# S4 convolution and attention: SP's transfers in the program's order, and other tiles over the bytes that transfers still read

## The chip, the cores and the metric

The kernel runs on one NeuronCore of a Trainium2 chip. The metric is the device time of one execution in microseconds (us); for a kernel that is run several times, the median. The core has these engines: TensorE (PE) multiplies matrices into PSUM, VectorE (DVE) and ScalarE (ACT) work on SBUF and PSUM, GpSimd (POOL) fills constants and issues some transfers, SyncE (SP) issues most of the DMA transfers. Each engine works through its own list of instructions in order and waits on semaphores.

## The reference, cut to what matters

Four layers, each added to its input: an S4 convolution (A), an attention with 32 query heads on one key and value head (B), and both again with the same parameters.

```python
def A(u, A_re, A_im, B_re, B_im, C_re, C_im, log_dt, Dskip):     # u: [1, 2048, 640]
    dt = exp(log_dt)[:, None]                                     # 640 channels, 128 states
    P = exp((dt * (A_re + 1j*A_im))[:, :, None] * arange(2048))
    K = einsum("dn,dnl,dn->dl", C_re + 1j*C_im, P, dt * (B_re + 1j*B_im)).real
    y = irfft(rfft(pad(u.T)) * rfft(pad(K)))[:, :2048].T          # causal convolution
    return y + u * Dskip
x = x + A(layernorm(x), ...)
x = x + B(layernorm(x), ...)      # softmax attention, 2048 x 2048, 32 heads of 20
x = x + A(layernorm(x), ...)
x = x + B(layernorm(x), ...)
```

## The kernel before, in words

The program has these stages in order: the generation of the convolution's kernels `K` (`_kgen`), the first convolution (names with `a`), attention (`b`), the second convolution (`c`), attention (`d`). The change touches the generation, and how the convolutions name their memory and load their weights.

**Tables** (`kg_tables`, L161 to L260). From the parameters, which are loaded as [128, 5, 128] tiles, DVE and ACT compute for every channel and state an angle `th`, its fraction `thr`, 32 times that (`th1`), a decay `are`, a phase `ph` and a logarithm of a size `lw`. Each of `th1`, `thr`, `are`, `ph`, `lw` is split into three bf16 parts, in a tile `h...` of [128, 3, 5, 128]: `cast` makes a part, `rest` subtracts it. PE needs them with 16 channels per group as rows, stacked: `tb` has the three parts of `th1` in 48 rows, `ta` has `thr` in rows 0 to 47 and `ph` in rows 48 to 95, `tm` has `are` and `lw` in the same way. Two ways of transfer bring them there:

- `send` (L183): one store of the tile to DRAM (`hd...`, L185) and, when that has landed, three loads of 16 rows each (L187). So go `th1` to `tb`, `thr` to `ta`, `are` to `tm`.
- the late ones (L292 to L297): for each of the 8 groups of 16 partitions of `hph` and of `hlw`, three transfers of 20 KB, straight into rows 48 to 95 of group `q` in `ta` and `tm`. These are 48 transfers, in the profile `ta<-hph` and `tm<-hlw`.

**Units** (L302 on). 20 units of work each take 32 channels: unit `u` reads group `u % 8` of the tables (`grp`). For a unit PE makes two phases (L324: the first from `tb`, the second from `ta`), DVE takes their fraction (`r` L149, `f` L329), ACT makes sines and cosines (`trig`, L342 to L344). PE makes three sizes (`sizes` L352: two from rows 0 to 47 of `tm`, the third from all 96), ACT takes their exponential into `m1` and `m2` (`exps`, L360 and L362). DVE multiplies (`products`, L370 to L379), PE sums over the states (`sums`, L388), ACT collects the sums in `kst` (`store`, L396). When `kst` is full, four transfers bring it to DRAM in `kd` (L404, L408).

**What sets the order.** The instructions of DVE, ACT and PE in this stage stand in the order in which the program writes them (`manual_schedule`). SP's are not among them: a planner at build time puts them in an order by its own estimate of when each is ready, and it also pulls later transfers forward, such as the loads of x (`load_x`, L531, written at unit 0). Each DMA of SP takes the next of eight semaphores and waits until the transfer that used it before has landed. The order in the loop for unit 0 on PE is: both phases of unit 0, two sizes of unit 0, the first phase of unit 1, the second phase of unit 1, the third size of unit 0. The PSUM buffer of the phases is single, that of the sizes double.

**Memory.** The tables' tiles lie in a pool `kgq`; when it closes, the pool `kgb` of the units takes the same bytes, and after that the convolution's pool `cvp`. Tiles get their bytes in the order in which the program names them (one set of buffers per tag). The first instruction that writes a tile waits until all that used its bytes before are done, transfers that read them included. In `kgq` the `h` tiles come late: each is named in `kg_tables`, after 25 other tiles. In `kgb` the order is `r` (2 buffers), `f` (4), `c1`, `s1` (2 each), `fa`, `c2`, `s2` (3 each), `m1` (3), `m2`, `e1r` (2 each), `kst`. In `cvp` it is `xn` (3 buffers; the kernel `kt` is one of them), `dsk`, `A` (3), `zs`, the scratch `B` and `R`, the inverse weights `wi`.

**Convolution** (`conv_layer`, L596). Per chunk of 128 channels: the kernel is loaded from `kd` (L588; in the second layer its spectrum `kh`, L585), the input is normalized on ACT (`xn`, L605), `fwd` multiplies with the weights `wf` on PE (L512: step `t` reads the parts `t + 4` and `t`) and does the rest of the transform on DVE with the scratch `B`, `R` (`fft8`). The weights are loaded in eight parts of 512 KB (L493).

Of the kernel before, what the change touches and what calls it, by code (L numbers as in the profile page):

```python
# [11 lines left out]
F32 = mybir.dt.float32  # L12
F32R = mybir.dt.float32r
BF16 = mybir.dt.bfloat16
# [7 lines left out]
P = 128  # L22
L = 2048
D = 640
NST = 128
# [92 lines left out]
class Net:  # L118
# [39 lines left out]
        with ExitStack() as ctx:  # L158
            self._kgen(ctx)

    def kg_tables(self, pp, t3, SH, ldt, aim, are_raw, bre, bim, cre, cim, ta, tb, tm):  # L161

        nc = self.nc
        V, S, T, A = (nc.vector.tensor_tensor, nc.vector.scalar_tensor_tensor, nc.vector.tensor_scalar,
                      nc.scalar.activation)
        dt, th, are, thr, th1, ph = pp.tile([P, 5], F32, name="dt"), *(
            t3(n) for n in ("th", "are", "thr", "th1", "ph"))
        wr, wi, u0, u1, u2, u3, lw = (t3(n) for n in ("wr", "wi", "u0", "u1", "u2", "u3", "lw"))  # L170
        ar, ai, mx, mn, gt = (t3(n) for n in ("ar", "ai", "mx", "mn", "gt"))
        hs, res = {}, {}
        for n in ("th1", "thr", "are", "ph", "lw"):
            hs[n] = pp.tile([P, 3, 5, NST], BF16, name="h" + n)
            res[n] = t3("res" + n)

        def cast(n, src, k):
            A(hs[n][:, k], src if k == 0 else res[n], AF.Copy)

        def rest(n, src, k):  # L180
            V(res[n], src if k == 0 else res[n], hs[n][:, k], ALU.subtract)

        def send(n, dst):  # L183
            hd = self.dr.tile([P, 3, 5 * NST], BF16, name="hd" + n)
            nc.sync.dma_start(hd, hs[n].rearrange("p k t s -> p k (t s)"))  # L185
            for k in range(3):
                nc.sync.dma_start(dst[16 * k : 16 * k + 16].rearrange("d q t s -> d q (t s)"),  # L187
                                  hd[:, k].rearrange("(q d) x -> d q x", d=16))

        A(dt, ldt, AF.Exp)  # L190
        for t in range(5):
            T(th[:, t], aim[:, t], dt[:, t : t + 1], 1.0 / TWO_PI, ALU.mult, ALU.mult)
        V(wr, cre, bre, ALU.mult)
        self.frac(pp, thr, th, SH)
        T(th1, thr, 32.0, None, ALU.mult)
        self.frac(pp, th1, th1, SH)
        cast("th1", th1, 0)
        V(u0, cim, bim, ALU.mult)
        V(wr, wr, u0, ALU.subtract)
        A(ar, wr, AF.Abs)  # L200
        V(wi, cre, bim, ALU.mult)
        V(u0, cim, bre, ALU.mult)
        V(wi, wi, u0, ALU.add)
        A(ai, wi, AF.Abs)
        rest("th1", th1, 0)
        cast("th1", th1, 1)
        V(mx, ar, ai, ALU.max)
        V(mn, ar, ai, ALU.min)
        T(mx, mx, 1e-37, None, ALU.max)
        rest("th1", th1, 1)  # L210
        cast("th1", th1, 2)
        send("th1", tb)
        cast("thr", thr, 0)
        nc.vector.reciprocal(u0, mx)
        V(u0, mn, u0, ALU.mult)
        for t in range(5):
            A(are[:, t], are_raw[:, t], AF.Copy, scale=dt[:, t : t + 1])
        cast("are", are, 0)

        A(u1, u0, AF.Arctan)  # L220
        V(gt, ai, ar, ALU.is_gt)
        rest("thr", thr, 0)
        cast("thr", thr, 1)
        T(wr, wr, 0.0, 0.5, ALU.is_lt, ALU.mult)
        S(u1, gt, 0.5 * math.pi, u1, op0=ALU.mult, op1=ALU.subtract)
        A(u1, u1, AF.Abs, scale=1.0 / TWO_PI)
        T(wi, wi, 0.0, -2.0, ALU.is_lt, ALU.mult)
        rest("thr", thr, 1)
        V(u1, wr, u1, ALU.subtract)
        A(u1, u1, AF.Abs)  # L230
        cast("thr", thr, 2)
        send("thr", ta)
        T(ph, th1, 32.0, None, ALU.mult)
        self.frac(pp, ph, ph, SH)
        S(u1, wi, 1.0, u1, op0=ALU.add, op1=ALU.mult)
        V(ph, ph, u1, ALU.add)
        self.frac(pp, ph, ph, SH)

        A(u2, u0, AF.Square)
        A(lw, mx, AF.Ln)  # L240
        A(u3, u2, AF.Ln, bias=1.0)
        nc.vector.tensor_copy(hs["ph"][:, 0], ph)
        rest("ph", ph, 0)
        nc.vector.tensor_copy(hs["ph"][:, 1], res["ph"])
        rest("ph", ph, 1)
        nc.vector.tensor_copy(hs["ph"][:, 2], res["ph"])
        rest("are", are, 0)
        cast("are", are, 1)
        S(lw, u3, 0.5, lw, op0=ALU.mult, op1=ALU.add)
        for t in range(5):  # L250
            T(lw[:, t], lw[:, t], ldt[:, t : t + 1], None, ALU.add)
        rest("are", are, 1)
        cast("are", are, 2)
        send("are", tm)
        nc.vector.tensor_copy(hs["lw"][:, 0], lw)
        rest("lw", lw, 0)
        nc.vector.tensor_copy(hs["lw"][:, 1], res["lw"])
        rest("lw", lw, 1)
        nc.vector.tensor_copy(hs["lw"][:, 2], res["lw"])
        return (ta, hs["ph"]), (tm, hs["lw"])  # L260

    def _kgen(self, ctx):
        tc, nc, ins = self.tc, self.nc, self.ins
# [10 lines left out]
        with tc.tile_pool(name="kgq", bufs=1) as pp:  # L274
            SH = [P, 5, NST]

            def t3(name):
                return pp.tile(SH, F32, name=name)

            ldt = pp.tile([P, 5], F32, name="ldt")  # L280
            nc.sync.dma_start(ldt, ins["A_log_dt"])
            raw = {}
            for n, eng in (("A_A_im", nc.sync), ("A_C_re", nc.scalar), ("A_B_re", nc.sync),
                           ("A_C_im", nc.scalar), ("A_B_im", nc.sync), ("A_A_re", nc.scalar)):
                raw[n] = t3("r" + n)
                eng.dma_start(raw[n], ins[n].rearrange("(t p) n -> p t n", p=P))
            nc.sync.dma_start(kg, ins["c_kg"])
            bre, bim, cre, cim = (raw["A_" + n] for n in ("B_re", "B_im", "C_re", "C_im"))
            with tc.manual_schedule(engines={mybir.EngineType.Activation, mybir.EngineType.DVE}):
                late = self.kg_tables(pp, t3, SH, ldt, raw["A_A_im"], raw["A_A_re"], bre, bim, cre, cim,  # L290
                                      ta, tb, tm)
            for q in range(8):  # L292
                for dst, h in late:
                    for k in range(3):
                        nc.sync.dma_start(
                            dst[48 + 16 * k : 64 + 16 * k, q].rearrange("d t s -> d (t s)"),
                            h[16 * q : 16 * q + 16, k].rearrange("d t s -> d (t s)"))  # L297

        bp = ctx.enter_context(tc.tile_pool(name="kgb", bufs=2, reuse_waits="tile"))

# [1 line left out]
        units = [(q, r, q * 256 + 16 * r, 128, 128) for q in range(2) for r in range(8)]  # L302
        units += [(2, r, 512 + 16 * r, 64, 64) for r in range(4)]
        C1, S1, C2, S2, M1, M2, E1R, F, PE_, PK, KST = ({} for _ in range(11))

        def big(tag, u, x, bufs=2):
            return bp.tile([P, 16, 2, x], F32, tag=tag, bufs=bufs, name=f"{tag}_{u}")
# [82 lines left out]

        def store(u):
            q, r, _, _, run = units[u]
            if r == 0:
                KST[q] = bp.tile([P, 32, run], F32, tag="kst", bufs=1, name=f"kst{q}")
            kst = KST[q]
            nc.scalar.activation(kst[:, :, 16 * r : 16 * r + 16],  # L396
                                 PK[u].rearrange("p (d j) -> p j d", d=16), AF.Copy)
            if 16 * (r + 1) == run:
                for par in range(2):
                    for jh in range(2):  # L400
                        src = kst[64 * par : 64 * par + 64, 16 * jh : 16 * jh + 16, :]
                        if run == 128:
                            dst = self.kd[2 * q + par, 64 * jh : 64 * jh + 64]
                            nc.sync.dma_start(dst, src.rearrange("p t d -> p (t d)"))  # L404
                        else:
                            dst = self.kd[4, 64 * jh : 64 * jh + 64].rearrange(
                                "p (t d) -> p t d", d=DC)[:, :, 64 * par : 64 * par + 64]
                            nc.sync.dma_start(dst, src)  # L408
# [68 lines left out]
    def conv_setup(self, ctx):  # L477
# [2 lines left out]
            self.conv_weights(self.nc.sync)  # L480
        self.cvp = ctx.enter_context(tc.tile_pool(name="cvp", bufs=1, reuse_waits="tile"))

    def conv_weights(self, eng):

        stack = ExitStack()
# [3 lines left out]
        self.wfs.append(stack)  # L489

    def load_weights(self, w, name, eng):
        for t in range(8):
            eng.dma_start(w[:, t].rearrange("p a b c k -> p (a b c k)"),  # L493
                          self.ins[name][:, t * 1024 : (t + 1) * 1024])

    def scratch(self, nm):
        cv = self.cvp
        return (cv.tile([P, 16, 256], F32, tag="B", bufs=1, name=f"B{nm}"),
                cv.tile([P, 8, 256], F32, tag="R", bufs=1, name=f"R{nm}"))
# [560 lines left out]
```

## Time and profile before

| | us |
|---|---|
| Median of 3 runs (3184.24 to 3188.92) | 3187.74 |
| The profiled execution's own time | 3188.56 |
| Its span, first to last instruction | 3186.5 |
| First matmul of the generation (L324) | starts at 31.89 |
| First sum collected (L396) | starts at 101.60 |
| First matmul of the first convolution (L512) | starts at 367.13 |

The times in the trace count from the first instruction. The difference between the profiled execution's time and its span lies outside the instructions. In a row of the timeline, the brackets behind an instruction hold how long its engine stood idle before it and what ended that; `<-` in a tile's place separates what is written from what is read. `x3` counts instructions that the view has merged. `SPq` is SP's list of DMA issues: the duration there is that of the issue, not of the transfer.

### The profile page before, as it was taken

How to read it: one execution, taken by the hardware profiler on the slowest of the kernel's cores; microseconds unless marked ns; L12 is line 12 of the kernel's file. 1: busy time of each engine (PE TensorE's matmuls, PEld its weight loads, DVE VectorE, ACT ScalarE, POOL GpSimd, SP SyncE). 2: the span in 40 equal slices, each digit the busy share in tenths (PEclk: the TensorE clock that was granted, in tenths of full speed). 3: DMA queues.
4: the chain of work that ended last, by engine and by line, in shares of the span. 5: the costliest groups of instructions: out<-in, count | busy, mean ns of one | idle time of the engine just before them, and what ended most of it. 6: DMA issues, size and time to landing. Idle time of an engine off the chain costs nothing. (4 is left out here: it accounts for less than half of the span.)

```text
span 3186.5 us, 51392 instructions
## 1 busy us (share of the span) xinstructions
PE 2790.6 (88%) x21374; PEld 1315.3 (41%) x21374; DVE 1375.5 (43%) x1699; ACT 2335.3 (73%) x2703; POOL 13.1 (0%) x60
## 2 busy tenths in 40 slices
PE   1888776649899999999999867388999999999999
PEld 0555676647522233333333467365222333333334
DVE  6888699994222122122222399953112212212222
ACT  3877411104599999999999630044999999999996
POOL 0000000000000000000000000000000000000000
PEclk9999988869999999999999988789999999999999
DMA  5110511012200000001001221123001111111111
GB/s 122 34 28 6 180 68 40 27 51 87 98 26 23 23 25 25 24 21 27 24 21 27 83 108 35 41 70 119 23 21 26 28 26 33 30 30 27 31 26 28
DMA packets 73379, 142.82 MB, mean 45 GB/s; under 512 B 22633, under 2 KB 28782, under 8 KB 70158
## 3 DMA queue, kind: packets, MB, share of 16 engines
q1 hardware_dynamic: 70018, 134.26, 14.3%
q8 instruction: 172, 2.82, 0.4%
q0 software_dynamic: 1152, 4.19, 0.3%
q10 hardware_dynamic: 1968, 0.98, 0.1%
q14 instruction: 69, 0.57, 0.1%
HBM read 82.52 MB, written 44.50 MB: 40 GB/s over the span
## 5 line engine op out<-in xcount | busy, mean ns | idle before, releaser
L870 ACT ACTIVATE pt<-scd 128x1024 f32<-128x1024 f32 x1024 | 941.4, 1201 | 7.1 <-PE scd L866 5.9
L870 ACT ACTIVATE pt<-scb 128x1024 f32<-128x1024 f32 x1024 | 941.4, 1201 | 6.9 <-PE scb L866 5.6
L880 PE MATMUL pod<-pt,vt 128*32 128x512 f32 x4096 | 546.4, 605 | 0.1
L880 PE MATMUL pob<-pt,vt 128*32 128x512 f32 x4096 | 546.4, 605 | 0.1
L866 PE MATMUL scd<-qpd,kt 62*128 62x512 f32 x2048 | 405.2, 462 | 5.4 <-DVEq L831 5.1
L866 PE MATMUL scb<-qpb,kt 62*128 62x512 f32 x2048 | 405.3, 462 | 5.4 <-DVEq L831 5.1
L866 PEld LDWEIGHTS scd<-qpd,kt 62*128 62x128 f32 x2048 | 173.4, 184 | 432.0 <-ACT pt L870 422.5
L866 PEld LDWEIGHTS scb<-qpb,kt 62*128 62x128 f32 x2048 | 173.3, 184 | 432.0 <-ACT pt L870 422.4
L935 DVE TENSOR_TENSOR x<-pyd,x 128x320 f32<-128x320 f32 x24 | 11.8, 492 | 476.3 <-PE pyd L917 476.3
L935 DVE TENSOR_TENSOR x<-pyb,x 128x320 f32<-128x320 f32 x24 | 11.8, 492 | 476.3 <-PE pyb L917 476.3
L897 DVE RECIPROCAL rc<-rc 128x512 f32<-128x512 f32 x64 | 214.6, 3353 | 2.2
L512 PE MATMUL zc<-xnc,wf 128*128 128x128 f32 x640 | 84.7, 301 | 73.6 <-DVE Ac L517 64.5
L880 PEld LDWEIGHTS pob<-pt,vt 128*32 128x32 f32 x4096 | 80.6, 108 | 160.8 <-issue 157.8
L880 PEld LDWEIGHTS pod<-pt,vt 128*32 128x32 f32 x4096 | 80.6, 108 | 160.7 <-issue 157.8
L638 PE MATMUL ya<-Aa,wi 128*128 128x128 f32 x640 | 82.7, 298 | 69.3 <-DVE Aa L106 69.3
L388 PE MATMUL pk<-s,m 128*64 128x32 f32 x1280 | 130.7, 295 | 12.6 <-DVE s L379 12.6
L388 PE MATMUL pk<-c,e1r 128*64 128x32 f32 x1280 | 132.1, 297 | 10.8 <-DVE c L378 10.6
L388 PEld LDWEIGHTS pk<-c,e1r 128*64 128x64 f32 x1280 | 105.2, 221 | 79.0 <-issue 52.5
L512 PE MATMUL zk<-kt,wf 128*128 128x128 f32 x640 | 84.0, 299 | 57.2 <-DVE Ak L517 43.7
L894 DVE COPY on<-pod 128x512 f32<-128x512 f32 x32 | 22.1, 692 | 256.9 <-PE pod L880 254.1
L894 DVE COPY on<-pob 128x512 f32<-128x512 f32 x32 | 22.1, 692 | 238.5 <-PE pob L880 226.0
L515 ACT ACTIVATE zsc<-zc 128x512 f32<-128x512 f32 x20 | 11.9, 595 | 148.9 <-DVE Ac L517 89.0
(331 smaller groups left out, 3254.0 us busy)
## 6 DMA issues: line engine op xcount, KB each, us to landing
kh<-Ak SPq DMA_DIRECT2D x5, 2048.0 KB
qhd<-qh SPq DMA_DIRECT2D x40, 256.0 KB
qld<-ql SPq DMA_DIRECT2D x40, 256.0 KB
qpb<-qhd SPq DMA_DIRECT2D x256, 40.0 KB
kh<-kh SPq DMA_DIRECT2D x5, 2048.0 KB
qpd<-qhd SPq DMA_DIRECT2D x256, 40.0 KB
ot<-on SPq DMA_DIRECT2D x224, 40.0 KB
wi<-in_c_wi SPq DMA_DIRECT2D x16, 512.0 KB
```

The lines of the kernel that those rows point to most:

```text
L388: nc.tensor.matmul(PK[u][64 * par : 64 * par + 64, 32 * d : 32 * d + 32], e[u][:, d, par], c[u][:, d, par], start=first, stop=not first)
L512: nc.tensor.matmul(zv[:, h, c, kk], self.wf[:, t + 4 * h, j, c, kk], xn[:, 8 * j + t + 4 * h], start=(j == 0), stop=(j == 1))
L515: nc.scalar.activation(zs, z[:, 512:1024], AF.Copy)
L638: nc.tensor.matmul(y[:, s * DC : (s + 1) * DC], self.wi[:, t, j, c_, kk], v[:, 2 * t + c_, kk], start=(i == 0), stop=(i == 3))
L866: nc.tensor.matmul(sc[:, 512 * par : 512 * par + 512], kt[rows, 128 * t : 128 * t + 128], qps[nb, hg, pr][rows], start=True, stop=True)
L870: nc.scalar.activation(pt, sc, AF.Exp, scale=SCALE)
L880: nc.tensor.matmul(po[32 * j : 32 * j + 32], vt[:, t], pts[step, j // 2][:, 512 * (j % 2) : 512 * (j % 2) + 512], start=(t == 0), stop=(t ...
L894: nc.vector.tensor_copy(on, po)
L897: nc.vector.reciprocal(rc, rc)
L935: nc.vector.tensor_tensor(xh, py, xh, ALU.add)
```

## The change

It does five things.

1. SP joins DVE and ACT in the manual schedule of the tables, so that its transfers there are issued in the order of the program. The late transfers move into `kg_tables`: those of `ph` for group 0 between the store of `are` and its three loads, then for each group those of `ph` and of `lw`.
2. The five `h` tiles are named first in the pool `kgq`, in the order `ph`, `lw`, `th1`, `thr`, `are`.
3. `kst` of the first round is named first in the pool `kgb`.
4. A first pair of scratch tiles `B`, `R` is named first in the pool `cvp`, and is used by the first `fwd`.
5. The eight parts of the weights are loaded in the order 0, 4, 1, 5, 2, 6, 3, 7.

```diff
-    def kg_tables(self, pp, t3, SH, ldt, aim, are_raw, bre, bim, cre, cim, ta, tb, tm):
+    def kg_tables(self, pp, hs, t3, SH, ldt, aim, are_raw, bre, bim, cre, cim, ta, tb, tm):
...
-        hs, res = {}, {}
-        for n in ("th1", "thr", "are", "ph", "lw"):
-            hs[n] = pp.tile([P, 3, 5, NST], BF16, name="h" + n)
-            res[n] = t3("res" + n)
+        res = {n: t3("res" + n) for n in hs}
...
-        def send(n, dst):
+        def send(n, dst, between=lambda: None):
             hd = self.dr.tile([P, 3, 5 * NST], BF16, name="hd" + n)
             nc.sync.dma_start(hd, hs[n].rearrange("p k t s -> p k (t s)"))
+            between()
             for k in range(3):
                 nc.sync.dma_start(dst[16 * k : 16 * k + 16].rearrange("d q t s -> d q (t s)"),
                                   hd[:, k].rearrange("(q d) x -> d q x", d=16))
+
+        def send_late(q, dst, h):
+            for k in range(3):
+                nc.sync.dma_start(dst[48 + 16 * k : 64 + 16 * k, q].rearrange("d t s -> d (t s)"),
+                                  h[16 * q : 16 * q + 16, k].rearrange("d t s -> d (t s)"))
...
-        send("are", tm)
+        send("are", tm, lambda: send_late(0, ta, hs["ph"]))
...
-        return (ta, hs["ph"]), (tm, hs["lw"])
+        for q in range(8):
+            if q > 0:
+                send_late(q, ta, hs["ph"])
+            send_late(q, tm, hs["lw"])
...
+            hs = {n: pp.tile([P, 3, 5, NST], BF16, name="h" + n)
+                  for n in ("ph", "lw", "th1", "thr", "are")}
             ldt = pp.tile([P, 5], F32, name="ldt")
...
-            with tc.manual_schedule(engines={mybir.EngineType.Activation, mybir.EngineType.DVE}):
-                late = self.kg_tables(pp, t3, SH, ldt, raw["A_A_im"], raw["A_A_re"], bre, bim, cre, cim,
-                                      ta, tb, tm)
-            for q in range(8):
-                for dst, h in late:
-                    for k in range(3):
-                        nc.sync.dma_start(
-                            dst[48 + 16 * k : 64 + 16 * k, q].rearrange("d t s -> d (t s)"),
-                            h[16 * q : 16 * q + 16, k].rearrange("d t s -> d (t s)"))
+            with tc.manual_schedule(engines={mybir.EngineType.Activation, mybir.EngineType.DVE,
+                                             mybir.EngineType.SP}):
+                self.kg_tables(pp, hs, t3, SH, ldt, raw["A_A_im"], raw["A_A_re"], bre, bim, cre, cim,
+                               ta, tb, tm)
...
+        KST[0] = bp.tile([P, 32, 128], F32, tag="kst", bufs=1, name="kst0")
...
-            if r == 0:
+            if r == 0 and q > 0:
                 KST[q] = bp.tile([P, 32, run], F32, tag="kst", bufs=1, name=f"kst{q}")
...
+        self.first = [self.new_scratch("0")]
...
-        for t in range(8):
+        for t in (0, 4, 1, 5, 2, 6, 3, 7):
...
     def scratch(self, nm):
+        return self.first.pop() if self.first else self.new_scratch(nm)
+
+    def new_scratch(self, nm):
```

## The prediction

> **What bounds the kernel now.** I began with the page, for the span and the shares of the engines:
>
> ```profile
> span 3186.5 us, 51392 instructions
> PE 2790.6 (88%) x21374; PEld 1315.3 (41%) x21374; DVE 1375.5 (43%) x1699; ACT 2335.3 (73%) x2703; POOL 13.1 (0%) x60
> PE   1888776649899999999999867388999999999999
> ```
>
> TensorE is busy almost everywhere except in the first slice of 80 us, and the change's transfers lie there. So I cut that start into windows (columns: PE, weight loads, DVE, ACT, POOL busy; granted clock; DMA share; GB/s), with a later stretch of the generation for comparison:
>
> ```profile
> core 0: us, PE busy (x) PEld busy (x) DVE busy (x) ACT busy (x) POOL busy (x), PEclk, DMA share, GB/s
> 0.00:20.00 20.00, 0.00 (x0) 0.00 (x0) 12.29 (x23) 4.44 (x6) 0.20 (x4) 1.00 0.95 223
> 60.00:70.00 10.00, 4.85 (x10) 1.17 (x11) 8.74 (x8) 4.46 (x5) 0.15 (x1) 1.00 0.13 32
> 70.00:80.00 10.00, 0.00 (x0) 0.00 (x0) 1.38 (x2) 0.06 (x1) 0.15 (x1) 1.00 0.12 32
> 80.00:90.00 10.00, 5.54 (x34) 2.21 (x35) 6.99 (x6) 9.75 (x10) 0.00 (x0) 1.00 1.07 254
> 200.00:250.00 50.00, 44.05 (x470) 27.09 (x472) 43.83 (x47) 37.00 (x39) 1.09 (x7) 1.00 0.20 43
> ```
>
> From 70 to 80 us all compute engines stand still while the DMA engines are 12% busy: this is neither work nor bandwidth. The timeline from 20 to 60 us says how it got there (start, duration, engine, line, out<-in; in brackets the idle time and what ended it):
>
> ```profile
> 4.53 2.70 SPq L531 DMA_DIRECT2D x<-in_A_u  x4
> 20.79 0.36 SPq L185 DMA_DIRECT2D hdth<-hth  x1
> 25.82 1.29 SPq L187 DMA_DIRECT2D tb<-hdth  x3
> 30.82 0.34 SPq L185 DMA_DIRECT2D hdthr<-hthr  x1
> 31.89 1.03 PE L324 MATMUL ph<-kg,tb 48*128 48x512 bf16 x2 [31.89 <-DMA tb<-hdth]
> 41.57 0.34 SPq L185 DMA_DIRECT2D hdare<-hare  x1
> 42.00 0.60 SPq L295 DMA_DIRECT2D ta<-hph  x1
> 42.66 1.54 SPq L187 DMA_DIRECT2D ta<-hdthr  x3
> 43.87 1.22 DVE L149 TENSOR_SCALAR r<-ph 128x1024 bf16<-128x1024 f32 x1
> 44.30 1.32 SPq L187 DMA_DIRECT2D tm<-hdare  x3
> 45.12 1.22 DVE L329 TENSOR_TENSOR f<-ph,r 128x1024 f32<-128x1024 f32 x1
> 45.66 1.17 SPq L295 DMA_DIRECT2D ta<-hph  x2
> 49.78 1.14 ACT L344 ACTIVATE c<-fa,halfpi 128x1024 f32<-128x1024 f32 x1
> 53.55 1.01 PE L324 MATMUL ph<-kg,ta 96*128 96x512 bf16 x2 [20.63 <-DMA tm<-hlw]
> 54.49 1.88 PE L352 MATMUL pe<-kg,tm 48*128 48x512 bf16 x4
> 54.60 1.23 DVE L149 TENSOR_SCALAR r<-ph 128x1024 bf16<-128x1024 f32 x1 [8.25 <-PE ph L324]
> 57.14 1.03 PE L324 MATMUL ph<-kg,tb 48*128 48x512 bf16 x2 [0.76 <-DVE f L329]
> 58.21 1.23 DVE L149 TENSOR_SCALAR r<-ph 128x1024 bf16<-128x1024 f32 x1 [1.12 <-PE ph L324]
> 60.23 1.28 ACT L360 ACT_TABLE_LOAD   x1
> ```
>
> SP stored `hdthr` at 30.82 and next had `hdare` in its list, which waits until 41.57 for ACT. Only behind that, at 42.66, come the loads of `ta` from `hdthr`. So the second phase of unit 0 starts on PE at 53.55, though its PSUM buffer was free at 46.34, when `f` of the first ended. DVE loses 8.25 us. Then the standstill:
>
> ```profile
> 70.16 1.22 DVE L376 TENSOR_TENSOR m<-m,s 128x1024 f32<-128x1024 f32 x1
> 76.84 1.78 SPq L295 DMA_DIRECT2D tm<-hlw  x3
> 79.94 1.94 ACT L360 ACTIVATE m<-pe 128x1024 f32<-128x1024 f32 x2 [15.26 <-DMA tm<-hlw]
> 81.01 1.01 PE L352 MATMUL pe<-kg,tm 96*128 96x512 bf16 x2 [14.42 <-ACT m L360]
> 82.91 1.23 DVE L149 TENSOR_SCALAR r<-ph 128x1024 bf16<-128x1024 f32 x1 [11.54 <-PE ph L324]
> 99.11 1.01 PE L352 MATMUL pe<-kg,tm 96*128 96x512 bf16 x2 [1.66 <-ACT m L360]
> 101.60 0.60 ACT L396 ACTIVATE kst<-pk 128x512 f32<-128x512 f32 x1 [0.41 <-PE pk L388]
> ```
>
> ACT's `m` of unit 1 waits 15.26 us for the last load out of `hlw`. It reads nothing of it: `m` only wants the bytes. Counting bytes per partition in the order of the calls, one of `m1`'s three buffers begins 82,432 above the pools' common base, and `hlw` lies at 84,544 to 88,384. PE's sizes wait for ACT (14.42), the phase of unit 2 queues behind them, DVE waits 11.54.
>
> **The change, part by part.** *Order on SP.* With the program's order, `hdthr` is followed by its three loads of `ta`. The store lands within the 2.73 us that passed from `hdare` (41.57) to its first load (44.30), or within the 5.03 that `hdth` took with loads of x ahead (20.79 to 25.82): the loads go out between 33.5 and 36. From the first load to the matmul that needs all three, `tb` shows 6.07 us (25.82 to 31.89): `ta` is filled by 42. Then `hdare` at 41.57, the three loads of `hph` for group 0 until about 43.8 (0.6 us each, as at 42.00), and `tm` from `hdare` at 44.3, as now. The loads of `hph` need some 2 us more, by 46. So PE can run the second phase when `f` ends at 46.34, 7.2 us before 53.55. What is late next? PE takes its matmuls in order, and behind the phase stand the two sizes of unit 0, which want `tm` from `hdare`: 44.3 + 6.07 = 50.4. They take 1.88, the first phase of unit 1 gives DVE its input 1.07 later (57.14 to 58.21), so DVE's `r` of unit 1 starts at 53.4 instead of 58.21: **4.8 us**. Bounds: if `tm` came at once, `f` of the second phase (46.34 + 1.07 + two passes of 1.23) and one more phase would hold it to 51.0, which is 7.2 us; if the store takes 5.03, it is 2.3 us less, 2.5.
>
> *The late sources' bytes.* The `h` tiles now come first in their pool and `kst` of group 0 first in the next: `hph`, `hlw`, `hth1` and `hthr` fill 15,360 of `kst`'s 16,384 bytes. Nothing of unit 1 lies over them. From `r` of unit 1, DVE runs without a wait worth naming to the end of L376: 58.21 to 71.38, 13.2 us. The next `r` then waits 11.54. That wait goes whole if ACT and PE keep ahead: ACT ends its first cosine at 50.9; the second trig (three like that cosine, 3.4), a table load (1.3) and one `m` (1.0) bring the first `m` to 56.6, while DVE needs it at 59.4 (53.4, four passes of 1.23, one phase). **11.5 us.** Who waits for the sources now? `kst`'s first write, at 101.60, after the change near 85. The sends: 45 after 45.6, at 1.78 for three, end near 73 and land by 76. Nine us are left; each us beyond them would stop ACT, and with it everything. The loads that each unit needs (six per group, 3.7 us) run ahead of the units: a unit is two PE and DVE streams at 88% of 50 us, some 14 us long. One thing gets a new wait: `hare` reaches past `kst` under `r`, so DVE's first `r` may wait for the store's landing, 44.3 instead of 43.87. That 0.4 is hidden by PE's wait until 50.4; without that cover it costs 0.4.
>
> *What follows the standstill.* At 99.11 PE still waits 1.66 us for ACT, which is catching up. After the change ACT's `m` of unit 1 comes behind the three of unit 0, at about 60 instead of 79.94, 20 us sooner, DVE's stream only 16; with this lead the wait goes. But PE is the busier engine in 200:250 by only 0.2 us before DVE, so DVE may keep the time. Between 0 and 1.7 I take the middle, **0.8 us**.
>
> *The convolution.* The rows of its start:
>
> ```profile
> 354.36 4.38 SPq L408 DMA_DIRECT2D kd<-kst  x4
> 358.84 1.45 SPq L588 DMA_DIRECT2D kt<-kd  x1
> 363.05 4.82 SPq L493 DMA_DIRECT2D wi<-in_c_wi  x8
> 367.13 16.86 PE L512 MATMUL zk<-kt,wf 128*128 128x128 f32 x128 [13.44 <-DMA kt<-kd]
> ```
>
> PE waits 13.44 us for `kt`, which is issued behind the stores of `kst`. `kt` does not lie over `kst` before or after; in the list before, `wi` does, and it is issued after `kt`. With `B` over `kst` instead, `wi` may go a little sooner, and `B` is first written some 15 us after 367.13, when the stores are long done. PE's wait stays: 0, unless SP's list changes (rival 3).
>
> *Order of the weights' parts.* In the second convolution the first matmuls need parts 0 and 4 of `wf`:
>
> ```profile
> 1825.02 27.22 PEld L512 LDWEIGHTS zc<-xnc,wf 128*128 128x128 f32 x224 [9.38 <-ACT xnc L605]
> ```
>
> At 1825.02 the normalized input arrives too, so an earlier part 4 gives at most one matmul's time: 0. For `wi` there is ample time.
>
> **Sum**: 4.8 + 11.5 + 0.8 = 17.1 us. The profiled execution took 3188.56, 2.1 more than its span; it becomes 3171.5. The median of the runs, 3187.74, is 0.8 below that execution: **3170.6 us**.
>
>
> **Rivals.**
> 1. *Loads of x slip into SP's waits.* SP now has to wait for each store in its order, and the loads of x, which are not part of that order, can be placed there, as four were at 4.53. At 223 GB/s one (64 partitions of 4 x 640 floats) takes 2.9 us. Before `ta`'s loads there is slack (42 against 46); before `tm`'s there is none, and one to four cost 2.9 to 11.5: 3173.5 to 3182.1. For: four of the eight were placed early before. Against: the three issues of `hph` stand between `hdare` and its loads, so little of a wait is left to fill.
> 2. *Slower: the bytes are not placed as I count.* The first tiles written, `r` and `f`, need 20 KB. If `kst`, named early and written late, did not take the lowest bytes, they would lie over `hph` and `hlw`, and DVE's first `r` would wait from 43.87 until all sends land, about 76. From there to `r` of unit 2 it is 20.3 us (51.0 + 13.2 - 43.87): 96.3 against 82.91, so 3201. It decides by one fact, whether any tile of unit 0 shares bytes with a late source. Against it: the count in call order places `m1` exactly over `hlw`, where the trace has the wait.
> 3. *`kt` is issued ahead of `kst`'s stores*, since bytes come free in another order: up to 13.4 us more, 3157. Against: `kt`'s bytes were free before, and SP's list still had it behind.
> 4. *Given back.* The convolutions' order on DVE and SP is not written out but planned; a plan with other bytes may lose 10 us or more of the 17: about 3183 to 3193. Nothing in the profile points to a place.
> 5. *TensorE comes slow out of a standstill.* PE was busy 5.54 us of the window after it; had it run there at half speed, half of that would go with the standstill: 2.8 us more, 3167.8. Against: the granted clock is 1.00 in 80:90 as everywhere, and two sizes take 1.01 at 81.01 as two phases did at 53.55.
>
> [...]
>
> **How the numbers follow.** Forecast 0.70; x 0.12; slower 0.04; `kt` early 0.04; given back 0.08; the slow TensorE 0.02. The forecast's own range: at most 7.2 + 11.5 + 1.7 = 20.4, at least 2.5 + 11.5 = 14.0, so 3167.3 to 3173.7; half the spread of the three runs (3184.24 to 3188.92) adds 2.3 on each side, 3165.0 to 3176.0. To keep only 2 in 10 outside, the upper end takes in one or two loads of x, 3178.5; the lower end I leave at 3165.5. A measurement of this kernel can tell 0.2%, 6.4 us, from no change. Faster by more: 0.70 + 0.04 + 0.02 + 0.11 = 0.87; within: 0.08 and 0.01 = 0.09; slower 0.04.
>
> **What would show it.** Right: SP's row `ta<-hdthr` right behind `hdthr`; DVE's second `r` near 47.5 and third near 53.4, that one waiting for PE, and PE for the loads of `tm`; no wait of ACT L360 for `hlw`; the window 70:80 as busy as 200:250; `kst` first written near 84.5; PE's 13.4 us before `zk` unchanged, near 350. Wrong: PE's third phase later than 55 (a load of x will stand ahead of `tm`'s); ACT L396 waiting for `hlw` (the sends end too late); DVE's first `r` far behind 44.3 (rival 2); a gain that is there at 90 us and smaller at 700 (rival 4).

## The result and the profile after

The kernel after takes 3170.96 us (median of 6 runs, 3169.35 to 3172.55), the kernel before 3188.07 (6 runs, 3184.24 to 3188.92). The ratio is 0.9948, with a 95% interval from 0.9935 to 0.9961: faster by 17.1 us, forecast 17.1; the interval allows 12.4 to 20.7. The terms of that sum are another matter. The profiled execution of after took 3171.06 us, 1.9 more than its span.

From the page of after, and from its windows over the start (columns as before: PE, weight loads, DVE, ACT, POOL busy; granted clock; DMA share; GB/s):

```profile
span 3169.2 us, 51393 instructions
PE 2787.7 (88%) x21374; PEld 1312.2 (41%) x21374; DVE 1375.2 (43%) x1699; ACT 2335.1 (74%) x2703; POOL 13.3 (0%) x60
```

```profile
70.00:80.00 10.00, 6.49 (x80) 4.55 (x82) 7.48 (x8) 9.89 (x11) 0.16 (x1) 1.00 0.12 30
80.00:90.00 10.00, 8.48 (x88) 4.98 (x86) 9.90 (x9) 5.15 (x6) 0.16 (x1) 1.00 0.49 126
200.00:250.00 50.00, 44.55 (x495) 28.27 (x496) 42.87 (x45) 38.62 (x40) 1.10 (x7) 1.00 0.01 1
```

The standstill is gone: in 70:80 ACT is busy for 9.89 of 10 us, where it had 0.06. Busy time in total has hardly changed (PE 2790.6 before, 2787.7 after). What went is waiting. The timeline of after, from 30 to 90 us, shows how:

```profile
30.46 0.34 SPq L182 DMA_DIRECT2D hdthr<-hthr  x1
30.85 0.47 SPq L541 DMA_DIRECT2D x<-in_A_u  x1
33.34 1.25 SPq L185 DMA_DIRECT2D ta<-hdthr  x3
41.22 0.34 SPq L182 DMA_DIRECT2D hdare<-hare  x1
41.65 1.87 SPq L190 DMA_DIRECT2D ta<-hph  x3
43.57 0.58 SPq L541 DMA_DIRECT2D x<-in_A_u  x1
43.90 1.23 DVE L149 TENSOR_SCALAR r<-ph 128x1024 bf16<-128x1024 f32 x1 [0.30 <-DMA hdare<-hare]
44.25 1.48 SPq L185 DMA_DIRECT2D tm<-hdare  x3
46.53 1.01 PE L329 MATMUL ph<-kg,ta 96*128 96x512 bf16 x2 [14.35 <-DVE f L334]
47.58 1.22 DVE L149 TENSOR_SCALAR r<-ph 128x1024 bf16<-128x1024 f32 x1 [1.19 <-PE ph L329]
53.39 1.86 PE L357 MATMUL pe<-kg,tm 48*128 48x512 bf16 x4 [5.84 <-DMA tm<-hdare]
56.14 1.23 DVE L149 TENSOR_SCALAR r<-ph 128x1024 bf16<-128x1024 f32 x1 [6.08 <-PE ph L329]
69.15 1.21 DVE L149 TENSOR_SCALAR r<-ph 128x1024 bf16<-128x1024 f32 x1
75.96 1.84 SPq L190 DMA_DIRECT2D tm<-hlw  x3
86.12 0.60 ACT L401 ACTIVATE kst<-pk 128x512 f32<-128x512 f32 x1 [0.41 <-PE pk L393]
```

SP now loads `ta` from `hdthr` at 33.34 instead of 42.66. PE's second phase starts at 46.53, when DVE's `f` ends (53.55 before; forecast 46.34). But at 43.57 a load of x stands between `hph` and the loads of `tm`. PE waits 5.84 us for `tm` and gets it at 53.39, not at 50.4, and DVE's first `r` of unit 1 follows at 56.14, not at 53.4. From there to the second `r` of unit 2 at 69.15 (82.91 before) DVE waits only once, 1.20 us for PE ahead of the second `r` of unit 1 (59.82). Then the start of the convolution:

```profile
339.43 4.38 SPq L413 DMA_DIRECT2D kd<-kst  x4
343.91 1.45 SPq L598 DMA_DIRECT2D kt<-kd  x1
352.00 16.56 PE L522 MATMUL zk<-kt,wf 128*128 128x128 f32 x128 [13.23 <-DMA kt<-kd]
```

`kt` is still issued behind the stores of `kst`, and PE waits 13.23 us for it (13.44 before). Further on, the two timelines give the gain as it stands at points of the program:

| | before | after | gain |
|---|---|---|---|
| DVE's first `r` of unit 1 | 58.21 | 56.14 | 2.07 |
| its second `r` of unit 2 | 82.91 | 69.15 | 13.76 |
| its first `r` of unit 4 | 107.33 | 92.81 | 14.52 |
| the last sum `pk` ends | 353.69 | 338.76 | 14.93 |
| first matmul of `zk` | 367.13 | 352.00 | 15.13 |
| the first convolution's last `ya` ends | 729.68 | 713.92 | 15.76 |
| first `pnb` (attention b, norms of the queries) | 745.38 | 727.72 | 17.66 |
| last `pob` ends (b's main loop) | 1795.54 | 1778.65 | 16.89 |
| the second convolution's last `yc` ends | 2095.01 | 2078.65 | 16.36 |
| first `pnd` (attention d) | 2110.68 | 2092.38 | 18.30 |
| last matmul (`pld`) ends | 3181.21 | 3163.89 | 17.32 |

So the generation gave 14.9, and 2.4 came behind it, mostly in two steps of 1.9 at the start of the attentions. The rows of the projections' matmuls there (a summary by tile: duration in ns, least/median/greatest, first and last start), before and then after:

```profile
L757 PE MATMUL pqd<-xh,wh x120: 388/396/669, 2101.6 to 2204.4; 128*128 128x512 f32 x100, 128*52 128x512 f32 x20
```

```profile
L767 PE MATMUL pqd<-xh,wh x120: 388/396/504, 2085.3 to 2186.1; 128*128 128x512 f32 x100, 128*52 128x512 f32 x20
```

And the windows around these first matmuls (the sixth column is the granted clock) with PE's timeline there (in brackets its idle time and what ended that), first before:

```profile
2095.00:2100.00 5.00, 3.10 (x20) 2.39 (x20) 3.54 (x19) 3.25 (x5) 1.05 (x3) 0.92 0.16 46
2100.00:2105.00 5.00, 3.87 (x11) 1.80 (x10) 2.95 (x3) 5.00 (x7) 0.00 (x0) 0.50 0.00 0
```

```profile
2098.48 2.01 PE L740 MATMUL ptd<-ident,x 128*128 128x128 f32 x11 [1.36 <-ACT x L731]
2101.62 0.67 PE L757 MATMUL pqd<-xh,wh 128*52 128x512 f32 x1 [1.13 <-DVE xl L661]
```

Then after:

```profile
2083.70:2088.70 5.00, 3.43 (x15) 1.92 (x16) 2.95 (x3) 4.90 (x7) 0.00 (x0) 1.00 0.00 0
```

```profile
2082.13 1.42 PE L750 MATMUL ptd<-ident,x 128*128 128x128 f32 x11 [1.36 <-ACT x L741]
2085.27 0.44 PE L767 MATMUL pqd<-xh,wh 128*52 128x512 f32 x1 [1.72 <-DVE xl L671]
```

Before, the clock falls to 0.50 at 2099.2, during the last transposes ahead of the projections (11 take 2.01 us, 1.42 after), and the first matmuls of the projections take up to 669 ns. After, it stays at 1.00, though PE's idle times there are no shorter. The forecast had nothing in this place.

### The profile page after: what moved, and what is told of

Same layout as the page of the kernel before. It is cut to its first block, busy times and chain, and to the rows that moved or that the text cites. A ratio compares the mean times of both kernels' runs of the same rounds, so it can differ in the third digit from the quotient of the medians.

```text
span 3169.2 us, 51393 instructions
## 1 busy us (share of the span) xinstructions
PE 2787.7 (88%) x21374; PEld 1312.2 (41%) x21374; DVE 1375.2 (43%) x1699; ACT 2335.1 (74%) x2703; POOL 13.3 (0%) x60
```

## The experiments

Theory: three terms add up in the generation (SP's order, the late sources' bytes, PE's wait for ACT), and the first came out 2.7 us short because of one load of x. Rivals: the loads of `tm` are slow by themselves; the order is worth something alone; the gain needs the other parts of the change. Each run is compared with runs of before on the same chip; these medians lie between 3186.5 and 3188.1.

**1. The loads of x behind the late sources** (`x_late`).

```diff
             send_late(q, tm, hs["lw"])
+        self.load_x()
...
-                    self.load_x()
```

> The kernel after, with the eight loads of x written behind the late sources, inside the program's order of SP. Theory (a load of x stands ahead of tm's loads and costs what the first term of the sum lacks): no load of x at 43.57, the three loads of tm from hdare go out by 43.6 to 44.3 and land by 50.4 instead of 53.25, DVE's first r of unit 1 starts near 53.4 instead of 56.14, and all that follows is 2.7 us earlier: 3168.3 us against 3170.96. Rival (tm's loads are slow by themselves, as 160 KB into 16 partitions each, and the load of x beside them is harmless): they land near 53, r of unit 1 stays near 56, time 3171. Second rival: the 2.7 us are gained at 53 us and are gone at 80 us, since the late sources now hold up the loads of x or kst: 3171, with a new wait of ACT or DVE between 56 and 110 us.

Measured: 3168.51 (5 runs; ratio 0.9945, 0.9932 to 0.9959). Timeline:

```profile
44.02 1.28 SPq L185 DMA_DIRECT2D tm<-hdare  x3
49.78 1.89 PE L358 MATMUL pe<-kg,tm 48*128 48x512 bf16 x4 [2.01 <-DMA tm<-hdare]
52.56 1.22 DVE L149 TENSOR_SCALAR r<-ph 128x1024 bf16<-128x1024 f32 x1 [2.27 <-PE ph L330]
```

`tm` is there 5.76 us after its first issue, at 49.78, and `r` of unit 1 comes at 52.56, 3.58 earlier than in after. The last sum ends 3.58 earlier too (335.18). The rival of slow loads is refuted. All runs of `x_late` (3166.55 to 3168.86) lie below all of after's, but those are from another chip: against before, the gains are 18.0 and 17.1, and their intervals overlap. It is the trace that shows the 3.6.

**2. Three loads of x ahead of `tm`** (`x_three`): the same, with `load_x` for parts 0 to 2 behind `send_late(0, ta, hs["ph"])`, the other five at the end.

> The kernel with all loads of x behind the late sources (x_late), but three of the eight put between the loads of hph for group 0 and the loads of tm from hdare, where after has one. Theory (each load of x there delays tm's loads by its own bytes, 3.58 us as between x_late and after, or 2.9 as by bytes): DVE's first r of unit 1, 52.56 in x_late and 56.14 in after, comes at 61.3 to 63.3, the first sums as much later, and the time is 3177 to 3179.3. Rival (the first load costs its start-up, the others only ride along): r of unit 1 below 58.5 and 3171 to 3174.5. Rival (the delay is caught up, since DVE and ACT have slack later): r of unit 1 late but the sums' end within 1 us of after: 3171.

Measured: 3177.17 (10 runs; ratio 0.9971, 0.9962 to 0.9981).

```profile
43.58 1.86 SPq L545 DMA_DIRECT2D x<-in_A_u  x3
45.54 1.53 SPq L185 DMA_DIRECT2D tm<-hdare  x3
59.23 1.86 PE L362 MATMUL pe<-kg,tm 48*128 48x512 bf16 x4 [11.66 <-DMA tm<-hdare]
61.98 1.22 DVE L149 TENSOR_SCALAR r<-ph 128x1024 bf16<-128x1024 f32 x1 [11.89 <-PE ph L334]
```

`tm`'s loads are issued only 1.5 us later than in `x_late` but are there 9.45 us later. So it is not SP's issue that costs: the data of x go ahead through the DMA engines, whose share is 0.94 to 1.14 in every 2 us from 45 to 57, where in `x_late` it is down to 0.13 from 49 on. `r` of unit 1 is 9.42 us later, 3.1 per load, and the last sum ends 9.5 later (344.70). Nothing is caught up.

**3. The order alone** (`order_alone`): the kernel before with SP in the manual schedule and the sends in `kg_tables` as in after; the tiles named where they were.

> The kernel before with only SP's order of after (stores with their loads, late sources by group), memory and weights' parts as before. Theory: PE's second phase comes at 46.5 and DVE's r of unit 1 at 56.1 instead of 58.2, but ACT's m of unit 1 still lies over hlw and waits until its last load has landed near 80.3; r of unit 2 (second, 82.91 before) comes at 82.5 to 83.5, so the order alone is worth 0: 3187.5 to 3188.5 us. Rival (the order is worth its 2 us wherever the bytes lie): 3186.

Measured: 3186.82 (11 runs), before 3186.52; ratio 1.0001, 0.9992 to 1.0010.

```profile
56.45 1.23 DVE L149 TENSOR_SCALAR r<-ph 128x1024 bf16<-128x1024 f32 x1 [6.43 <-PE ph L329]
79.32 1.94 ACT L365 ACTIVATE m<-pe 128x1024 f32<-128x1024 f32 x2 [17.31 <-DMA tm<-hlw]
82.29 1.22 DVE L149 TENSOR_SCALAR r<-ph 128x1024 bf16<-128x1024 f32 x1 [12.76 <-PE ph L329]
```

The 1.8 us gained at 56.45 are waited away: ACT's wait for `hlw` grows from 15.26 to 17.31, and the second `r` of unit 2 comes at 82.29, 0.62 sooner than before. As expected, the order by itself is worth nothing that can be timed. It pays only once no tile of the units lies over a late source.

**4. The bytes alone** (`bytes_alone`): the kernel before with the two namings.

```diff
+            hs = {n: pp.tile([P, 3, 5, NST], BF16, name="h" + n)
+                  for n in ("ph", "lw", "th1", "thr", "are")}
...
+        KST[0] = bp.tile([P, 32, 128], F32, tag="kst", bufs=1, name="kst0")
```

> The kernel before with only the sources' tiles named first and kst of group 0 named first; SP's order, the convolution's scratch and the weights' parts as before. Theory: r of unit 1 stays at 58.2, no wait of ACT for hlw, second r of unit 2 near 71.4 instead of 82.91 (11.5 us), the wait of PE for ACT near 99 goes (0.7): 12.2 us by the end of the generation. If the rest of the kernel gains nothing of its own, 3175.9 us. Rival (the 2.7 us that after gained behind the generation come with any shift of this stage): 3173 to 3174. Rival (they come from the other parts of the change, scratch or weights' parts): 3175.9.

Measured: 3173.49 (5 runs; ratio 0.9959, 0.9946 to 0.9973), 13.0 below before; by the end of the generation 12.2 were expected, and the trace has 13.1.

```profile
57.84 1.22 DVE L149 TENSOR_SCALAR r<-ph 128x1024 bf16<-128x1024 f32 x1 [1.13 <-PE ph L324]
70.92 1.21 DVE L149 TENSOR_SCALAR r<-ph 128x1024 bf16<-128x1024 f32 x1
```

From 57.84 to 70.92 is 13.08 us; before it was 58.21 to 82.91. So 11.6 us belong to the bytes, and the last sum ends 13.1 earlier (340.55). In after it ends at 338.76: there the order adds the 1.8 us that it was not worth alone. In this profile the projections have their slow start in both attentions (9.09 and 9.07 us from the first `pq` to the first `pn`), as before.

**5. `kst` not first** (`kst_old`): the kernel after with `KST[0]` named in `store`, as before. It prices the forecast's second rival.

> The kernel after with kst of group 0 named at its old place, behind the units' other tiles. Theory (what the change gains hangs on which tile lies over the late sources): r and f of unit 0 lie over hph and hlw, DVE's first r waits from 43.9 until the last of them has landed near 80, and from there it is 20 to 25 us to the second r of unit 2: 100 to 105 instead of 69.15; time 3202 to 3206 us, slower than before by 14 to 18. Rival (the pool gives the lowest bytes to the first tiles in the list but the release is per group, so only a few sends count): first r near 55, time near 3180.

Measured: 3201.88 (4 runs; ratio 1.0050, 1.0034 to 1.0065): slower than before by 15.4.

```profile
77.58 1.22 DVE L149 TENSOR_SCALAR r<-ph 128x1024 bf16<-128x1024 f32 x1 [33.72 <-DMA ta<-hph]
99.58 1.21 DVE L149 TENSOR_SCALAR r<-ph 128x1024 bf16<-128x1024 f32 x1
```

DVE's very first `r` waits 33.72 us for the sends of `hph`, and the second `r` of unit 2 follows 22.0 behind it. One line that names a tile decides between 17 us of gain and 15 of loss.

**6. Without the convolution's scratch first** (`no_scratch`): the kernel after with `self.first = []`.

> The kernel after without the convolution's scratch named first; order, sources' tiles, kst first and weights' parts as after. Theory (this part is worth nothing but keeps kt off kst): kt now lies over kst and its load waits until the stores of kst have landed, so PE's wait ahead of zk grows from 13.23 to 15 to 19 us and the time is 3172.5 to 3177. Rival (kt waits for these stores anyway, since it reads what they write): zk's wait stays at 13.2, 3171. On what after gained behind the generation: in the profile of after the first matmuls of the projections take 7.12 us from the first pq to the first pn where before and bytes_alone have 9.08, in both attentions, with 1 us given back in each main loop. If the scratch's place causes that, 9.1 comes back here, about 2 us more in all; if the weights' parts do, 7.1 stays.

Measured: 3172.81 (5 runs; ratio 0.9961, 0.9947 to 0.9974).

```profile
347.89 0.34 SPq L598 DMA_DIRECT2D kt<-kd  x1
352.71 16.87 PE L522 MATMUL zk<-kt,wf 128*128 128x128 f32 x128 [13.72 <-DMA kt<-kd]
```

`kt` does wait for the stores, 4.0 us at its issue (343.91 in after), yet it lands only about half a microsecond later behind the sums: 13.72 against 13.23. My 15 to 19 were wrong: in after too `kt`, issued behind the stores of `kst`, comes only when they are out of the way, it seems, however soon behind them it is issued. Attention b has its slow start again (9.04), d has not (7.06).

**7. and 8. The weights' parts alone** (`wparts`) **and the scratch alone** (`scratch_alone`): the kernel before with one of the two.

> The kernel before with only the weights loaded in the order 0, 4, 1, 5, 2, 6, 3, 7. Theory of the prediction: part 4 comes earlier but the second convolution gains at most one matmul, 0 us in all: 3186.5 to 3188. What the profile of after suggests beside it: the first zc comes 26.3 us after the attention instead of 29.5, 3.2 sooner, and yc 57.2 after zc instead of 53.9, so that all of it is given back inside the convolution. If the weights' parts also set the projections' start (7.1 instead of 9.1 from pq to pn, less 0.8 to 1.0 in each main loop), the time is 2 us lower, 3184.5 to 3186; if not, 0.

> The kernel before with only the convolution's first scratch named first. Theory of the prediction: B takes the place over kst, wi goes elsewhere, PE's wait ahead of zk stays at 13.4, and nothing changes: 3186.5 to 3188. Rival (this part is what makes the projections start at 7.1 instead of 9.1 us, less 0.8 to 1.0 in each main loop): 3184.5 to 3186. Second rival (tiles move and the planned order of the convolutions with them, so that 10 us or more are lost): above 3195.

Measured: 3186.28 (11 runs; ratio 1.0001, 0.9992 to 1.0010) and 3185.59 (11 runs; ratio 0.9999, 0.9990 to 1.0008). Neither can be told from no change. In the profile of `wparts` the second convolution starts as said:

```profile
1820.59 0.80 PE L512 MATMUL zc<-xnc,wf 128*128 128x128 f32 x2 [5.94 <-ACT xnc L605]
```

That is 26.28 us behind the attention instead of 29.51, and `yc` begins 56.64 behind that instead of 53.88: 2.8 of the 3.2 us are given back inside the convolution. Attention d then starts fast (7.06), b does not (9.06). With the scratch alone both start fast (7.03 and 7.06). These two parts move the time at which the attentions begin; experiment 9 shows how the clock there hangs on that. A net 1 us each is inside the interval.

**9. More transposes** (`turn_more`): the kernel before, with work that is not needed in PE's idle time ahead of the projections.

```diff
-                            nc.tensor.transpose(pt[:, 512 * k + 128 * i : 512 * k + 128 * i + 128],
-                                                xs[i][:, 128 * (k0 + k) : 128 * (k0 + k) + 128], self.ident)
+                            for _ in range(1 if nb > 0 or k0 == 4 or k == 1 else (2, 2, 4, 1)[i]):
+                                nc.tensor.transpose(pt[:, 512 * k + 128 * i : 512 * k + 128 * i + 128],
+                                                    xs[i][:, 128 * (k0 + k) : 128 * (k0 + k) + 128], self.ident)
```

> The kernel before, with the first transposes of each attention done over again while PE waits for x there (the parts of the first two tiles twice, of the third four times, the same values to the same place): work that is not needed, put into idle time of about 2 us ahead of the projections. Theory (the slow first matmuls of the projections, 0.43 us each for 4 us at a granted clock of 0.5, come from PE's idle time ahead of them): they run at 0.23 us, pq to pn is 7.1 instead of 9.06 us in both attentions, 0.8 to 1.0 of each is given back in the main loop: 2 us less in the profile, 3185 to 3186.5 at before's 3187.7. Rival (the rate has another cause, as weights that arrive late): 9.06 stays, and the time is that of before or up to 2 us more.

Measured: 3185.22 (10 runs; ratio 0.9993, 0.9984 to 1.0002). The same windows as above:

```profile
2092.90:2097.90 5.00, 4.08 (x30) 3.15 (x30) 3.54 (x19) 3.25 (x5) 1.06 (x3) 1.00 0.17 46
2097.90:2102.90 5.00, 3.39 (x16) 1.87 (x16) 2.95 (x3) 4.94 (x7) 0.00 (x0) 1.00 0.01 3
```

With PE busy for 4.08 of the 5 us instead of 3.10, the granted clock stays at 1.00, and from the first `pq` to the first `pn` it is 7.03 and 7.11 us in the two attentions instead of 9.08 and 9.06. That alone does not show the cause: in the profiles of the other 13 kernels, 16 of the 26 attentions start at full clock without any added work, with PE busy for only 2.98 to 3.06 us of these 5, and the other ten start at half clock.

What separates them is the place in time. In every trace, each stretch at one granted clock that lies between two changes lasts 3.41 us or a multiple of it (in before and after all 76: 3.41, 6.83, 10.24, 13.65 and more), so the changes lie on a grid. Counted from the last point of this grid, the first transpose of an attention starts at 0.27 to 0.30 or at 1.99 to 2.33 us in the 16 starts at full clock, and at 1.16 to 1.17 or at 2.52 to 2.63 us in the ten at half clock. In `turn_more` attention b starts at 2.64, beside the eight from 2.52 to 2.63, and its clock does not fall. So there the added work took the fall away, though in one start of one profile; d starts at 2.26, where the others keep the full clock too. So the start at half clock hangs on the place in the grid and, as far as this one start shows, on PE's idle time there.

The time is unclear, as 2 us in 3187 would be. The fall came without a long idle time of PE: before's timeline shows 3.10 of 5 us busy and no idle time over 1.36 ahead of it. Why one place in the grid brings it and another does not is not shown.

**10. to 12. The first `kt` on another queue.** The third rival of the forecast had `kt` ahead of `kst`'s stores, at up to 13.4 us. GpSimd's queue is free there (its last transfers in after, those of the weights `wf`, land by 334.0 us):

```diff
-        nc.sync.dma_start(kt.rearrange("p t d -> p (t d)"), self.kd[c])
+        eng = nc.gpsimd if c == 0 else nc.sync
+        eng.dma_start(kt.rearrange("p t d -> p (t d)"), self.kd[c])
```

`kt_pool` does this in after, `x_late_kt` in `x_late`; `x_late_kt_dsk` puts the load of `dsk` on `eng` too.

> The kernel after with the first load of kt issued by GpSimd instead of SyncE, so that it no longer stands behind the last stores of kst in SP's list (its data were stored by about 210 us, its bytes are free by about 330). It measures the price of the prediction's third rival, up to 13.2 us. Theory (PE's wait of 13.23 ahead of zk is only SP's order): kt lands before 340 and zk starts at 340 to 342 instead of 352.00, when PSUM is free; the work behind it on DVE and ACT has no other wait of that size, so 10 to 12 us come through: 3159 to 3161. Rival (the first convolution is bound by DVE, which has the statistics of x until about 345): zk starts at 341, but za's first part of the chain on DVE gains only some 5 us: 3166. Rival (GpSimd's issue waits for something else, as the weights' loads do): zk at 350, 3170.

> The kernel with both: the loads of x behind the late sources and the first kt issued by GpSimd. Theory (two waits on different stretches add): x_late's 3168.5 less what the first kt on GpSimd gives to after, 10 to 12 us: 3156.5 to 3158.5. Rival (one swallows part of the other): above 3160.

> As x_late_kt, with the first load of dsk issued by GpSimd too. In kt_pool zk starts at 339.17, at once behind the sums, but its second group of matmuls waits 5.75 us for DVE's sum of kt and dsk (348.37), and that for dsk, which SP issues at 344.40 behind the last stores of kst and which lands at 348.28. Theory (what is late next is dsk alone): no wait of PE between the sums and the end of zk, some 5.7 us earlier, less what ACT and DVE have to do there: 3164.45 less 4 to 5.7 is 3158.7 to 3160.5. Rival (the first results of zk wait for ACT, which has the statistics and xna until 349 and gives zs only behind it): 3163 to 3164.5.

Measured: 3168.30 (5 runs; ratio 0.9938, 0.9924 to 0.9952), 3164.45 (5 runs; 0.9924, 0.9910 to 0.9937) and 3166.44 (5 runs; 0.9934, 0.9921 to 0.9948). First the timeline of `kt_pool`:

```profile
339.17 3.78 PE L522 MATMUL zk<-kt,wf 128*128 128x128 f32 x16
344.40 1.34 SPq L601 DMA_DIRECT2D dsk<-in_A_Dskip  x1
348.37 0.28 DVE L602 TENSOR_TENSOR kt<-kt,dsk 1x128 f32<-1x128 f32 x1 [5.63 <-DMA dsk<-in_A_Dskip]
348.71 13.48 PE L522 MATMUL zk<-kt,wf 128*128 128x128 f32 x94 [5.75 <-DVE kt L602]
```

`zk` starts 12.83 us earlier than in after, behind the sums without a wait. But its second group needs the sum of `kt` and `dsk`, and `dsk`, one row of 512 bytes, now comes last in SP's list. At the end of the first convolution 1.8 of the 12.8 us are left (712.09 against 713.92). In `x_late_kt` the same edit leaves 2.6 of 13.1 there (706.98 against 709.59 in `x_late`). With `dsk` moved as well, the second fault shows:

```profile
347.39 0.39 SPq L599 DMA_DIRECT2D kt<-kd  x1
359.75 0.28 DVE L602 TENSOR_TENSOR kt<-kt,dsk 1x128 f32<-1x128 f32 x1 [11.73 <-DMA kt<-kd]
```

The planner has now put the sum for the second chunk ahead of the rest of the first on DVE, and its `kt` is issued at 347.39, behind the eight parts of `wi`. DVE waits 11.73 us, and the first convolution ends at 708.61, later than in `x_late_kt`. All three expectations of 4 to 12 us were wrong in size, the last one, by the traces, in sign (the ratios' intervals of the last two overlap). `x_late_kt` is the fastest version here: 23.3 us below before. All its runs (3161.08 to 3164.96) lie below all runs of after, which are from another chip; the intervals of the two ratios just overlap.

## Why the prediction came out

**Term 1, the order on SP: the step that failed.** 4.8 us forecast, 2.07 measured (58.21 to 56.14). The working held in every step but one: `ta` in time, PE's second phase at 46.53 (46.34), DVE's second `r` at 47.58 (47.5), `r` of unit 1 bound by `tm` from `hdare`. Wrong was "44.3 + 6.07 = 50.4", with nothing else on the way. The first rival, given 0.12, is what happened, with one load of x. The argument against it (little of a wait is left to fill) was about room in time, where the planner's list decides: what isn't in the written-out order can be put anywhere between. Without that load the step is right: `tm` took 5.76 us instead of 6.07, and `r` came at 52.56, forecast 53.4. The price of a load there was 2.9 us by bytes; it measured 3.6 for one and 3.1 each for three.

**Term 2, the bytes.** The count holds: `m1`'s third buffer begins at 82,432, with one buffer of `fa` in the kernel and not three, as the description of the memory can be read. 11.5 forecast. 69.15 less 56.14 is 13.01, before it was 24.70: 11.69, and 11.6 in `bytes_alone`. The sends ended later than I said (SP's last group at 75.96 ends at 77.8, forecast 73, since SP took 4.99 us for one group of three at 47.60). `kst`'s first write at 86.12 still came 8.3 behind that, without a wait for them. The new wait of DVE's first `r` for `hare` is there, 0.30 (0.4), and hidden behind PE's wait.

**Term 3.** 0.8 forecast, 0.76 measured (14.52 less 13.76). PE's wait of 1.66 us for ACT is gone: the same two sizes start at 83.61 without one.

**Convolution and weights.** Forecast 0 each; 0.21 at `zk`, and no difference that can be timed for `wparts`. The second convolution's earlier start (3.2 us) I had put at one matmul at most; it is given back inside.

**Total.** The generation gives 14.9 and not 17.1. That the time is the forecast's is in part luck: 2.7 us were missing in the first term, and 2.4 came behind the generation, where the sum had nothing. The two steps of 1.9 us at the attentions are luck too: before's starts lie at 2.62 and 2.61 us of the clock's grid (experiment 9), after's at 0.29 and 2.03. The change moved them there without aiming at it, and in `x_three` and `kt_pool` the slow start is back in d (9.74 us each from the first `pq` to the first `pn`). The main loops give back 0.77 and 0.98 us in after (from the first `pn` to the last `po` 1050.16 to 1050.93 in b, from the first `pn` to the last `pl` 1070.53 to 1071.51 in d); why is open.

How often a kernel's attentions start at half clock is open too, for each has one profile. Of the other runs only the time and the mean granted clock are on record. Two such starts, at 0.50 for 6.83 us each, would lower that mean by an estimated 0.002. Before's profiled run, with two, has 0.955; of the 66 runs of before beside the experiments, 41 have 0.955 (median 3187.4) and 14 have 0.957 (median 3185.5). That would fit a fall of the clock that comes and goes between runs of one kernel.

**The other rivals.** The second was priced nearly rightly: 13.4 us slower than before against 15.4, since the wait ended later (77.58 for 76) and what follows took 22.0 us for 20.3. The third was overpriced: `kt` early is worth 1.8 to 2.6 us in the traces (2.3 and 5.3 in the differences to before) and not 13.4, because `dsk` and DVE's list are late next. The fourth did not occur. The fifth did not occur behind the standstill, but its counter-argument, the granted clock of 1.00, was a misreading. The traces have no clock record before the first convolution (in before the first is at 372.0 us, in after at 356.2), and the view shows 1.00 where there is none. The first matmuls of `zk` in before, on the two sides of that point:

```profile
368.00:371.00 3.00, 3.00 (x16) 3.00 (x16) 0.00 (x0) 0.00 (x0) 0.00 (x0) 1.00 1.04 412
373.00:376.00 3.00, 3.00 (x29) 3.00 (x28) 1.29 (x2) 0.60 (x1) 0.00 (x0) 1.00 1.04 419
```

Their starts lie mostly 213 ns apart until 372.0 and 112 ns from there; later in before, matmuls of this line lie 213 ns apart where the record has 0.50 and 112 ns where it has 1.00. So TensorE ran at half rate into the first convolution, and in after `zk` has the same 213 and 112 ns. In the whole generation a matmul of 512 columns takes some 0.62 us, ahead of the standstill and behind it, in both kernels. The standstill therefore cost no clock, and the sum is not touched. That the generation too ran at half rate is an estimate, from the projections' matmuls of 512 columns, which take 0.63 us at a clock of 0.50 and 0.39 at 1.00: those are of f32, the generation's of bf16. Why the rate would be low there, with PE busy for 44 of 50 us in 200:250, is open.

## What to carry to other kernels

Before writing out an engine's order, list what stays outside it, for a planner can put exactly that into the one place without slack. Where early transfers read from memory that is used again, ask which tile comes to lie over them and when it is first written: the reuse was worth 11.6 us here, the order of the transfers nothing without it. When a total agrees, check the sum at each stage, for two misses of opposite sign look like a hit.

## What the runs showed of the hardware

TensorE's granted clock fell to 0.50 after a stretch in which PE was busy for 3.10 of 5 us with no idle time over 1.36, and stayed at 1.00 with idle times of 1.36 and 1.72 in another kernel. What differs is the place in the grid of the clock's changes, which lie 3.41 us or a multiple of it apart (experiment 9). A fall lasted 6.83 us in all ten starts that had one and made the way from the first `pq` to the first `pn` 2.0 us longer, in two of them 2.7.

A granted clock of 1.00 in a window without a clock record says nothing: the distance of like matmuls does (213 ns and 112 ns for `zk`, both shown as 1.00).

A transfer that SP issues 4.0 us later (`kt` in `no_scratch`) made PE wait only 0.5 us longer, and loads issued 1.5 us later behind three loads of x landed so that PE started 9.45 us later: the time of issue says little where other data are ahead.
